# A Fourier mixer and a SoLU layer on one core: the order of the opening's transfers, and the buffers and transfers of the last pairs

## The chip, the core and the metric

The kernel runs on one core of one Trainium2 chip. The time is device microseconds of one launch. The kernel before took 1618.07 us in the median of three runs (1616.99 to 1626.45); a profiled execution of it took 1612.3 us. Five engines work side by side, each through its own list of instructions in order: TensorE (PE, with PEld for its weight loads), VectorE (DVE), ScalarE (ACT), GpSimd (POOL) and SyncE (SP), which only issues transfers. They wait for one another through semaphores. In these traces a line such as L858 is a line of the kernel before.

## What is computed

```
X = np.fft.rfft(x, axis=1)                     # x: 8 x 3136 x 256
Y = X * (filt_r + 1j * filt_i)[None, :, :]
y = np.fft.irfft(Y, n=3136, axis=1)            # 25088 tokens of 256
h = y @ w_in                                   # 256 -> 1024
e = np.exp(h - max(h)); sm = e / (sum(e) + 1e-9)
solu = h * sm
ln = (solu - mean(solu)) / sqrt(var(solu) + 1e-6) * g_ln
out = ln @ w_out                               # 1024 -> 256
```

All in float32. `w_in`, `w_out` and `g_ln` come as float64 and are converted on the chip.

## The kernel before

**Two halves that overlap.** Each of the eight sequences is a Fourier transform of length 3136 = 49 x 64, done as products with small tables. A first product per piece (`first`, eight pieces of four columns) goes through a tensor in DRAM (`d1`) to change its layout. The spectrum is then treated in seven units (`Spectrum.units`): six of four rows and a last one of a single row. For each unit `forward` makes two PSUM tiles `pb`, `multiply` multiplies them by the filter into `pr` and `pi` (VectorE, with one sum on GpSimd), `inverse` makes `pc`, ScalarE copies it to `g`, and `store` writes `g` to `d2` in DRAM. A last product per piece (`back`, tiles `py`) reads `d2` back as `t4` and leaves tokens in `y`.

Tokens go in blocks of 128, two blocks to a pair, 98 pairs. `product` makes `h` (tiles `m`), `exponential`, `normalize`, `square` and `turn` make the SoLU and its transposed blocks (`turn`), `regroup` moves these by DMA into `solu_t`, `project_sums` makes the sums of `solu_t` that a product scheme of seven instead of eight blocks needs (`u1`, `u2`, the sum written over `solu_t`, `u4`; all on GpSimd), and `project` makes the seven products 1, 2, 6, 7, 5, 3, 4 of a pair into the PSUM tiles `o`. Between them `keep_out` (ScalarE, L871) and `finish_out` (VectorE, L875) empty the banks into `ot`, and `store_out` writes `ot` to the output. Products 6, 5 and (except in the last pairs) 3 add to the bank of product 1, so each waits for the `keep_out` before it; product 4 adds to the bank of 2 and 7 and waits for a `finish_out`.

**The opening.** Sequence 0 has nothing to overlap with. Everything stands in an order written by hand (`manual_schedule`). SP's transfers there are, in order: eight parts of unit 0's rows (L563), the rows of units 1 and 2 (`y<-d`, L295, 512 KB each, into a free part of `y`), the last tables (`load_tables(8, ...)`: `de`, 640 KB, and eight filter pieces of 128 or 160 KB), the rows of units 3 to 6, and then `t4` in eight pieces. ScalarE issues the stores of `g`; GpSimd issues the raw weights (`begin`, 512 KB each) one after each unit's sum. In the loop over the units, TensorE runs `forward` two units ahead: pb of unit 3, pc of unit 1, pb of unit 4, pc of unit 2 and so on. The tiles `pr`, `pi` and `g` have two buffers each. After the last unit fourteen products whose results nobody reads (`idle_row(14, "idler")`) keep TensorE running until the first `t4` piece is there. Each `t4` piece has 100 rows: 96 from units 0 to 5 and 4 from unit 6, and `by_16` fetches them as two transfers.

**The semaphores of transfers.** In the built program the transfers of SP and ACT share eight semaphores in turn. Each transfer carries a wait for the landing of the one that used its semaphore before it; the issuing engine stands at that wait.

**The end.** `last` holds the pairs 93 to 97. Their stores are issued by GpSimd, except those of pair 97 (SP). `ot` has two buffers, so pair 96 uses that of pair 94. SP regroups pairs 96 and 97 one after the other in step k = 198; pair 97 uses two of the four buffers of pool `r`.

Of the kernel before, what the change touches and what calls it, by code (L numbers as in the profile page):

```python
# [9 lines left out]
FP32 = mybir.dt.float32  # L10
# [7 lines left out]
P = 128  # L18
B, S, C = 8, 3136, 256
# [6 lines left out]
NS, NQ = (N1 + 1) // 2, 64  # L26
NP = (NS + 1) // 2
NR = 2 * N1
NK = 4 * NS
# [65 lines left out]
def kernel(  # L95
# [31 lines left out]
    d1 = [dram.tile([NS, P, C], FP32, name=f"d1_{e}") for e in range(B)]  # L127
    d2 = [dram.tile([NS, P, C], FP32, name=f"d2_{e}") for e in range(B)]
    f_dram = dram.tile([NP, 2, NQ, 2, C], FP32, name="f_dram")

# [57 lines left out]
    class Spectrum:  # L188
# [156 lines left out]
        def store(self, i, dma):  # L345
            rows, n = self.rows(i, d2[self.e])
            dma(out=rows, in_=self.gs.pop(i)[:, 0:n, :])

    t4s = {}

    def fetch_first_back(ch):
        by_16((nc.sync.dma_start, nc.sync.dma_start), t4s[0, ch],
              d2[0].rearrange("s (a n) c -> (s a) n c", a=4)[:, NCH * ch:NCH * ch + NCH, :])

# [51 lines left out]
    with ExitStack() as st:  # L406
# [158 lines left out]
        for i in range(1, units):  # L565
            sp.fetch(i, nc.sync.dma_start, spare_piece(i - 1))
            if i == 2:
                load_tables(8, NP - 8, nc.sync.dma_start)
        for i in range(2):
            start(i)  # L570
        for i in range(units):
# [13 lines left out]
            elif i != 2:  # L585
                begin({1: 2, 3: 3, 4: 4, 5: 5, 6: 6}[i])
        idle_row(14, "idler")
        rows_t4 = pools["r"].tile([P, NH, C], FP32, name="t4_0", tag="r")
# [96 lines left out]
    def load_de(sp, u):  # L685
# [5 lines left out]

    turns, variances, solu_ts, solu_sums, spreads, rss, pos, ots, places = (
        {} for _ in range(9))
    sums, ms, hs, nmaxs, es, solus, squares = {}, {}, {}, {}, {}, {}, {}
# [99 lines left out]

    def regroup(p, i):


        g, second = divmod(p, 2)
        turned = turns[g].rearrange("p (k q) b i -> p k q (b i)", q=4)
        a = 2 * second + i  # L800
        if p == last[-1]:
            st = pools["r"].tile([P, KF, P], FP32, name=f"solu_t_{p}_{i}", tag="r")
        else:
            st = upool.tile([P, KF, P], FP32, name=f"solu_t_{p}_{i}", tag=f"solu_t{i}")
        solu_ts[p, i] = st[:, 0:KF // 2, :], st[:, KF // 2:KF, :]
        for q in range(4):
            nc.sync.dma_start(out=st[32 * q:32 * q + 32, :, :],  # L807
                              in_=turned[32 * a:32 * a + 32, :, q, :])

# [54 lines left out]
    def out_half(p, i, n):  # L864
        if p not in ots:
            ots[p] = wk2.tile([P, 2, C], FP32, name=f"ot_{p}", tag="ot")
        return ots[p][:, i, P * n:P * n + P], rss[p // 2][:, 2 * (p % 2) + i:2 * (p % 2) + i + 1]
# [10 lines left out]
    def store_out(p):  # L878
        g, second = divmod(p, 2)

        rows = out[4 * P * g:4 * P * g + 4 * P, :].rearrange("(b a i) c -> a b i c", a=4, i=32)
        for i in range(2):
            (nc.gpsimd if p in last[:-1] else nc.sync).dma_start(out=rows[2 * second + i], in_=ots[p][:, i, :])
        del ots[p]
# [79 lines left out]
    def step(k):  # L964
# [23 lines left out]
        if not odd:  # L988
# [37 lines left out]
            if 0 <= j - 3 < pairs - 1:  # L1026
                for n in range(j - 3, pairs if j - 3 == pairs - 2 else j - 2):
                    regroup(n, 0)
                    regroup(n, 1)
            if 0 <= j - 4 < pairs:  # L1030
# [16 lines left out]
        else:  # L1047
# [6 lines left out]
            if proj:  # L1054
                project(p, 1)
                keep_out(p, 0, (0, 0))
                project(p, 2)
                finish_out(p, 0, 0, (0, 0), 1)
# [17 lines left out]
            if proj:  # L1076
                keep_out(p, 1, (1, 0))
            if 3 <= k < blocks + 3:
                square(k - 3)
# [45 lines left out]
```

## Time and profile before

| what | us |
|---|---|
| median of three runs | 1618.07 |
| the profiled execution | 1612.3 |
| its span, first to last instruction | 1610.2 |
| mean granted clock of TensorE | 0.991 of full |

| stretch of the span, us | length | PE busy | granted clock | DMA share |
|---|---|---|---|---|
| 0 to 53: first products, tables, unit 0 | 53.0 | 33.17 | 0.90 | 0.94 |
| 53 to 105: units 1 to 6, unread products, `back` | 52.0 | 45.47 | 0.93 | 0.80 |
| 105 to 142: the first steps | 37.0 | 33.15 | 0.96 | 0.79 |
| 142 to 1571.8: the steps | 1429.8 | 1412.28 | 1.00 | 0.69 |
| 1571.8 to 1605.5: the last three pairs | 33.7 | 28.57 | 0.90 | 0.43 |

PE busy is the time in which TensorE has a product in flight; the granted clock is the share of the full clock that the throttle let through; the DMA share is the mean busy share of the core's 16 DMA engines. A wait in a profile is written as waiting engine and line, arrow, what ended the wait. A letter q behind an engine is its issuing part: SPq L807 is SP issuing a transfer. Between the span and the execution's time lie 2.1 us.

### The profile page before, as it was taken

The numbers are of one execution on the slowest core, as the hardware profiler recorded it, in microseconds if no ns is written. First come the engines' busy times: TensorE is split into PE (matmuls) and PEld (weight loads), VectorE is DVE, ScalarE is ACT, GpSimd is POOL, SyncE is SP. The second block draws the span as 40 slices with busy tenths as digits, with TensorE's granted clock in tenths as the row PEclk, the third lists the DMA queues.
The fourth block names the chain that finished last, engine by engine and source line by source line (L and its number), as shares of the span: only waits on it lengthen the run. The fifth ranks groups of instructions, "written<-read, shape, count | busy, mean of one in ns | idle before, by whom it ended". The sixth has DMA issues, their size and how long they took to land.

```text
span 1610.2 us, 37028 instructions
## 1 busy us (share of the span) xinstructions
PE 1552.6 (96%) x12808; PEld 1057.4 (66%) x12808; DVE 1316.2 (82%) x2635; ACT 913.2 (57%) x1821; POOL 1196.3 (74%) x1386
## 2 busy tenths in 40 slices
PE   5798899999999999999999999999999999999997
PEld 1362456666666676667766676667767777777776
DVE  1687887898899889987999789987898777777772
ACT  2135555566656656666565655666555665666662
POOL 4446998679777876886778877797776767677775
PEclk8999999999999999999999999999999999999999
DMA  9888878786887679866886678766774545344343
GB/s 274 245 267 246 251 219 237 210 228 199 216 258 235 180 200 257 236 181 164 229 240 206 169 194 254 202 189 176 219 222 125 141 118 133 86 113 110 106 112 99
DMA packets 342651, 311.94 MB, mean 194 GB/s; under 512 B 28922, under 2 KB 307987, under 8 KB 342467
## 3 DMA queue, kind: packets, MB, share of 16 engines
q1 hardware_dynamic: 268724, 167.37, 39.5%
q0 software_dynamic: 35648, 102.76, 21.1%
q10 hardware_dynamic: 38096, 39.46, 8.2%
q8 instruction: 104, 1.70, 0.5%
q14 instruction: 79, 0.65, 0.1%
HBM read 124.78 MB, written 81.40 MB: 128 GB/s over the span
## 4 chain that ended last, share of the span: by engine, by line
PE 66%; DMA 2%; DVE 1%; issue 1%; POOL 0%; SPq 0%; ACT 0%; DVEq 0%; POOLq 0%; ACTq 0%
PE o L858 30%; PE m L728 28%; PE py L376 3%; PE pc L305 2%; PE pa L273 2%; PE pb L305 2%; DMA solu_t<-turn 1%; DMA x<-in_x_dram 1%; DVE h L776 0%; DMA out_dram<-ot 0%; PE o L822 0%; DVE h L752 0%; SPq L807 0%; POOL u L707 0%; DVE h L749 0%
## 5 line engine op out<-in xcount | busy, mean ns | idle before, releaser
L858 PEld LDWEIGHTS o<-w_out_sb,solu_t 128*128 128x128 f32 x3136 | 382.4, 192 | 49.6 <-issue 43.5
L858 PE MATMUL o<-w_out_sb,solu_t 128*128 128x128 f32 x3136 | 402.2, 276 | 3.4 <-DVE ot L875 2.6
L728 PE MATMUL m<-w_in_sb,s 128*128 128x512 f32 x784 | 398.0, 608 | 3.4 <-ACT h L738 1.6
L858 PEld LDWEIGHTS o<-w_out_sb,u 128*128 128x128 f32 x2352 | 307.5, 192 | 141.8 <-issue 105.4
L776 DVE SCALAR_TENSOR_TENSOR h<-e,rsum,h 128x1024 f32<-128x1024 f32 x196 | 320.5, 1635 | 6.9
L858 PE MATMUL o<-w_out_sb,u 128*128 128x128 f32 x2352 | 311.8, 276 | 4.9 <-ACT ot L871 4.8
L728 PE MATMUL m<-w_in_sb,y 128*128 128x512 f32 x588 | 308.4, 608 | 5.0 <-DVE nmax L752 3.5
L738 ACT COPY h<-m 128x512 f32<-128x512 f32 x294 | 173.2, 589 | 203.3 <-PE m L728 194.2
L871 ACT ACTIVATE ot<-o,rs_t 128x128 f32<-128x128 f32 x392 | 143.2, 367 | 253.3 <-PE o L858 244.0
L707 POOL TENSOR_TENSOR u<-solu_t 128x512 f32<-128x512 f32 x98 | 137.8, 1406 | 165.5 <-DMA solu_t<-turn 114.5
L784 ACT ACTIVATE h<-h,nmu 128x1024 f32<-128x1024 f32 x196 | 224.8, 1147 | 48.6 <-DVE turn L792 38.1
L792 DVE STREAM_TRANSPOSE turn<-h 128x1024 f32<-128x1024 f32 x196 | 243.1, 1240 | 3.1
L752 DVE CUSTOM_DVE_ANT_0 h<-m,h 128x512 f32<-128x512 f32 x196 | 133.3, 680 | 128.1 <-ACT h L738 97.9
L760 ACT ACTIVATE e<-h,nmax 128x1024 f32<-128x1024 f32 x196 | 225.1, 1148 | 21.2 <-DVE h L776 19.8
L707 POOL TENSOR_TENSOR u<-solu_t,u 128x512 f32<-128x512 f32 x98 | 149.2, 1522 | 93.6 <-PE o L858 93.6
L728 PEld LDWEIGHTS m<-w_in_sb,s 128*128 128x128 f32 x784 | 127.8, 190 | 88.8 <-issue 67.1
L875 DVE SCALAR_TENSOR_TENSOR ot<-o,rs_t,ot 128x128 f32<-128x128 f32 x299 | 103.7, 347 | 78.4 <-ACT ot L871 59.9
L707 POOL TENSOR_TENSOR solu_t<-solu_t,solu_t 128x512 f32<-128x512 f32 x98 | 165.9, 1693 | 0.9
L728 PEld LDWEIGHTS m<-w_in_sb,y 128*128 128x128 f32 x588 | 96.6, 191 | 101.6 <-issue 55.6
L707 POOL TENSOR_TENSOR u<-u,solu_t 128x512 f32<-128x512 f32 x98 | 150.8, 1538 | 15.6 <-PE o L858 8.1
L707 POOL TENSOR_TENSOR s<-y 128x128 f32<-128x128 f32 x196 | 96.5, 493 | 0.5
L376 PEld LDWEIGHTS py<-wb_t,t 50*64 50x64 f32 x3584 | 57.6, 134 | 42.9 <-issue 19.4
(123 smaller groups left out, 2020.6 us busy)
## 6 DMA issues: line engine op xcount, KB each, us to landing
solu_t<-turn SPq DMA_DIRECT2D x784, 128.0 KB
out_dram<-ot SPq DMA_DIRECT2D x188, 128.0 KB
t<-d POOLq DMA_DIRECT2D x112, 200.0 KB, 6.9
d<-x POOLq DMA_DIRECT2D x100, 200.0 KB, 5.6
f<-f_dram POOLq DMA_DIRECT2D x39, 512.0 KB, 8.1
d<-g POOLq DMA_DIRECT2D x39, 512.0 KB, 5.0
t<-d ACTq DMA_DIRECT2D x37, 512.0 KB
x<-in_x_dram SPq DMA_DIRECT2D x112, 98.0 KB
```

The lines of the kernel that those rows point to most:

```text
L376: nc.tensor.matmul(out=views[g][64 * h:64 * h + 64, cb, i, :], lhsT=t4[rows, i, c0:c0 + 64], rhs=wb_t[rows, 0:N1], start=True, stop=True)
L707: nc.gpsimd.tensor_tensor(out=out, in0=in0, in1=in1, op=op)
L728: nc.tensor.matmul(out=ms[j, bank], lhsT=lhsT, rhs=w_in_sb[:, w, :], start=m in (1, 2, 7), stop=True, skip_group_check=True)
L738: nc.scalar.copy(out=h_half(k, i), in_=ms[j, 0])
L752: nc.vector.tensor_tensor_reduce(out=h_half(k, i), in0=ms[j, bank], in1=h_half(*kept), scale=1.0, scalar=sofar, op0=ALU.add, op1=ALU.min, ...
L760: nc.scalar.activation(out=e, in_=hs[k], func=AFT.Exp, bias=nmaxs.pop(k)[:, 1:2], scale=-1.0, accum_out=esum)
L776: nc.vector.scalar_tensor_tensor(out=solu, in0=e, scalar=rsum, in1=solu, op0=ALU.mult, op1=ALU.mult, accum_out=nmu)
L784: nc.scalar.activation(out=solu, in_=solu, func=AFT.Square, bias=nmu, scale=-float(DFF), accum_out=variances[g][:, i:i + 1])
L792: nc.vector.transpose(out=turns[g][:, :, i, :], in_=solus[k].rearrange("p (f j) -> p f j", j=32))
L858: nc.tensor.matmul(out=pos[p, bank], lhsT=lhs[:, f, :], rhs=w[:, f, :], start=f == 0 and (m in (1, 2, 7) or alone), stop=True, skip_group_ ...
L871: nc.scalar.activation(out=out_half(p, *to)[0], in_=pos[p, 0], func=AFT.Copy, scale=rs)
L875: nc.vector.scalar_tensor_tensor(out=ot, in0=pos[p, bank], scalar=rs, in1=out_half(p, *kept)[0], op0=ALU.mult, op1=ALU.add)
```

## The change

It has two places.

In the opening, the last tables are issued when i is 3, so after the rows of units 1, 2 and 3. The last unit's result goes to a DRAM tensor of its own, `d2_last`. `fetch_first_back` takes the 96 rows from `d2` and the four from `d2_last`, and for the first two pieces the order is: 96 rows of piece 0, 96 of piece 1, four of piece 0, four of piece 1. Eleven unread products stand where fourteen stood.

At the end, all stores are issued by SP, those of pairs 93 to 96 too. `ot` of pairs 96 and 97 comes from pool `r`. `regroup` can do some of its four parts and on another queue: SP regroups pairs 96 and the first block of 97; the four parts of the second block of 97 are issued by ScalarE in step k = 199, two behind the `keep_out` of product 1 of pair 95, and two behind that of its product 6. In the built program nothing else moves on any engine, and the number of transfers is the same: four fewer pairs of stores on GpSimd, four more on SP, four parts of a regroup on ScalarE instead of SP.

```diff
@@ -126,6 +126,7 @@
 
     d1 = [dram.tile([NS, P, C], FP32, name=f"d1_{e}") for e in range(B)]
     d2 = [dram.tile([NS, P, C], FP32, name=f"d2_{e}") for e in range(B)]
+    d2_last = dram.tile([1, P, C], FP32, name="d2_last")
     f_dram = dram.tile([NP, 2, NQ, 2, C], FP32, name="f_dram")
 
     wf_t = consts.tile([NR, NK], FP32, name="wf_t")
@@ -344,13 +345,18 @@
 
         def store(self, i, dma):
             rows, n = self.rows(i, d2[self.e])
+            if self.e == 0 and n == 1:
+                rows = d2_last.rearrange("s p c -> p s c")
             dma(out=rows, in_=self.gs.pop(i)[:, 0:n, :])
 
     t4s = {}
 
     def fetch_first_back(ch):
-        by_16((nc.sync.dma_start, nc.sync.dma_start), t4s[0, ch],
-              d2[0].rearrange("s (a n) c -> (s a) n c", a=4)[:, NCH * ch:NCH * ch + NCH, :])
+        for rest in range(2):
+            d, place = ((d2[0][0:NS - 1], slice(0, NK - 4)), (d2_last, slice(NK - 4, NK)))[rest]
+            for n in ([0, 1] if ch == 0 else [ch] if ch > 1 else []):
+                nc.sync.dma_start(out=t4s[0, n][place], in_=d.rearrange("s (a n) c -> (s a) n c", a=4)[
+                    :, NCH * n:NCH * n + NCH, :])
 
     def fetch_back(e, ch):
 
@@ -564,7 +570,7 @@
                 out=t2_0[NH * (n % 4):NH * (n % 4) + NH, n // 4, :], in_=rows_x[n:n + 1])
         for i in range(1, units):
             sp.fetch(i, nc.sync.dma_start, spare_piece(i - 1))
-            if i == 2:
+            if i == 3:
                 load_tables(8, NP - 8, nc.sync.dma_start)
         for i in range(2):
             start(i)
@@ -584,7 +590,7 @@
                 nc.gpsimd.dma_start(out=g_sb, in_=moe_g_ln.rearrange("(k p) -> p k", p=P))
             elif i != 2:
                 begin({1: 2, 3: 3, 4: 4, 5: 5, 6: 6}[i])
-        idle_row(14, "idler")
+        idle_row(11, "idler")
         rows_t4 = pools["r"].tile([P, NH, C], FP32, name="t4_0", tag="r")
         for ch in range(pieces):
             t4s[0, ch] = rows_t4[0:NK, NCH * ch:NCH * ch + NCH]
@@ -689,8 +695,8 @@
                             in_=de_dram[i:i + pairs].rearrange("i p k u q -> p i (k u q)"))
         return de
 
-    turns, variances, solu_ts, solu_sums, spreads, rss, pos, ots, places = (
-        {} for _ in range(9))
+    turns, variances, solu_ts, solu_sums, spreads, rss, pos, ots, places, regrouped = (
+        {} for _ in range(10))
     sums, ms, hs, nmaxs, es, solus, squares = {}, {}, {}, {}, {}, {}, {}
 
 
@@ -792,20 +798,21 @@
         nc.vector.transpose(out=turns[g][:, :, i, :],
                             in_=solus[k].rearrange("p (f j) -> p f j", j=32))
 
-    def regroup(p, i):
+    def regroup(p, i, dma=nc.sync.dma_start, parts=range(4)):
 
 
         g, second = divmod(p, 2)
         turned = turns[g].rearrange("p (k q) b i -> p k q (b i)", q=4)
         a = 2 * second + i
-        if p == last[-1]:
-            st = pools["r"].tile([P, KF, P], FP32, name=f"solu_t_{p}_{i}", tag="r")
-        else:
-            st = upool.tile([P, KF, P], FP32, name=f"solu_t_{p}_{i}", tag=f"solu_t{i}")
-        solu_ts[p, i] = st[:, 0:KF // 2, :], st[:, KF // 2:KF, :]
-        for q in range(4):
-            nc.sync.dma_start(out=st[32 * q:32 * q + 32, :, :],
-                              in_=turned[32 * a:32 * a + 32, :, q, :])
+        if (p, i) not in regrouped:
+            if p == last[-1]:
+                st = pools["r"].tile([P, KF, P], FP32, name=f"solu_t_{p}_{i}", tag="r")
+            else:
+                st = upool.tile([P, KF, P], FP32, name=f"solu_t_{p}_{i}", tag=f"solu_t{i}")
+            regrouped[p, i] = st
+            solu_ts[p, i] = st[:, 0:KF // 2, :], st[:, KF // 2:KF, :]
+        for q in parts:
+            dma(out=regrouped[p, i][32 * q:32 * q + 32, :, :], in_=turned[32 * a:32 * a + 32, :, q, :])
 
     def deviations(g):
         rs = small.tile([P, 4], FP32, name=f"rs_{g}", tag="rs", bufs=2)
@@ -863,7 +870,10 @@
 
     def out_half(p, i, n):
         if p not in ots:
-            ots[p] = wk2.tile([P, 2, C], FP32, name=f"ot_{p}", tag="ot")
+            if p in last[-2:]:
+                ots[p] = pools["r"].tile([P, NCH, C], FP32, name=f"ot_{p}", tag="r")[:, 0:2]
+            else:
+                ots[p] = wk2.tile([P, 2, C], FP32, name=f"ot_{p}", tag="ot")
         return ots[p][:, i, P * n:P * n + P], rss[p // 2][:, 2 * (p % 2) + i:2 * (p % 2) + i + 1]
 
     def keep_out(p, i, to):
@@ -880,7 +890,7 @@
 
         rows = out[4 * P * g:4 * P * g + 4 * P, :].rearrange("(b a i) c -> a b i c", a=4, i=32)
         for i in range(2):
-            (nc.gpsimd if p in last[:-1] else nc.sync).dma_start(out=rows[2 * second + i], in_=ots[p][:, i, :])
+            nc.sync.dma_start(out=rows[2 * second + i], in_=ots[p][:, i, :])
         del ots[p]
 
     blocks = NT * B // 2
@@ -1026,7 +1036,8 @@
             if 0 <= j - 3 < pairs - 1:
                 for n in range(j - 3, pairs if j - 3 == pairs - 2 else j - 2):
                     regroup(n, 0)
-                    regroup(n, 1)
+                    if n != last[-1]:
+                        regroup(n, 1)
             if 0 <= j - 4 < pairs:
                 project_sums(j - 4, 1)
             if 0 <= j - 3 < pairs and j % 2:
@@ -1054,6 +1065,9 @@
             if proj:
                 project(p, 1)
                 keep_out(p, 0, (0, 0))
+            if j == pairs + 1:
+                regroup(last[-1], 1, nc.scalar.dma_start, range(2))
+            if proj:
                 project(p, 2)
                 finish_out(p, 0, 0, (0, 0), 1)
             if 2 <= k < blocks + 2:
@@ -1075,6 +1089,8 @@
                 normalize(k - 2)
             if proj:
                 keep_out(p, 1, (1, 0))
+            if j == pairs + 1:
+                regroup(last[-1], 1, nc.scalar.dma_start, range(2, 4))
             if 3 <= k < blocks + 3:
                 square(k - 3)
             for job in first_parts[k]:
```

## The prediction

> **What bounds the kernel now.** I read the page first: how busy each engine is, then the chain of work that ended last.
>
> ```profile
> PE 1552.6 (96%) x12808; PEld 1057.4 (66%) x12808; DVE 1316.2 (82%) x2635; ACT 913.2 (57%) x1821; POOL 1196.3 (74%) x1386
> ...
> PE 66%; DMA 2%; DVE 1%; issue 1%; POOL 0%; SPq 0%; ACT 0%; DVEq 0%; POOLq 0%; ACTq 0%
> ```
>
> TensorE is busy 96% of 1610.2 us. The change leaves every product of the long middle as it is, so only stretches in which TensorE stands still, or runs slowly, can move the time. The busy time by windows shows two of each (columns: window, its length, busy time of PE, PEld, DVE, ACT, POOL with instruction counts, granted clock, DMA share, GB/s).
>
> ```profile
> 53.00:57.80 4.80, 0.07 (x2) 0.02 (x1) 4.53 (x7) 1.07 (x2) 3.38 (x6) 0.90 0.89 266
> 57.80:63.70 5.90, 5.89 (x38) 2.71 (x42) 0.00 (x0) 0.00 (x0) 1.18 (x1) 0.50 0.84 282
> ...
> 1586.80:1591.30 4.50, 0.00 (x0) 0.00 (x1) 0.08 (x1) 0.37 (x1) 4.50 (x5) 0.80 0.74 192
> 1591.30:1596.30 5.00, 4.97 (x23) 5.00 (x24) 0.27 (x1) 0.37 (x1) 2.83 (x3) 0.50 0.36 88
> ```
>
> Each stop of 4.5 to 4.8 us is followed by 5 to 6 us at half clock. A stop therefore costs its length plus about half of the slow stretch: 4.7 + 2.9 = 7.6 us in the opening, 4.5 + 2.5 = 7.0 us at the end. These 14.6 us are the most that the change can win. Who ends them, from the waits of the opening (us in total, times, longest) and the timeline of the end:
>
> ```profile
> SPq L295 <- DMA d<-g: 9.2, 1, 9.2
> ```
>
> ```profile
> PE pb L305 <- DMA y<-d: 4.7, 1, 4.7
> ```
>
> ```profile
> 1583.85 1.45 POOL L883 DMA_DIRECT2D out_dram<-ot  x2
> ...
> 1590.82 0.37 ACT L871 ACTIVATE ot<-o,rs_t 128x128 f32<-128x128 f32 x1 [5.74 <-DMA out_dram<-ot]
> ...
> 1591.33 2.05 PE L858 MATMUL o<-w_out_sb,u 128*128 128x128 f32 x8 [4.56 <-ACT ot L871]
> ```
>
> The first stop waits for the rows of unit 3 (`y<-d`). SP issues them at 52.89, behind the last tables (42.60 to 52.85). The second is a buffer: `ot` of pair 96 needs the store of pair 94, which POOL issues only at 1583.85, after its sums and `rs`, `wide`, and which lands at 1590.6.
>
> [...] 0.50 from 56.89 to 63.71 and from 1589.47 to 1596.30, and a stop of 1.84 us at 136.7 inside a thin stretch also cost 3.41 us at half. [...] a regroup part from SP lands 2.4 us after its issue alone, and 4.8 to 6.5 us after it beside POOL's stores. [...] in the trace ACT's copies of `g` stand behind waits on their stores (4.4 us).
>
> **The change, part by part**
>
> *Unit 3's rows ahead of the tables.* SP issues y3 at 42.60, in the place of `de`. Units 1 and 2 (512 KB each) land at 46.5 and 47.9, 1.44 us apart, so y3 lands near 49.3. Pair product pb of unit 3 then follows pc of unit 0 at 53.1 instead of 57.8: **4.7 us earlier and at full clock**. What it is moved past is 1.4 us later: `de` and eight filter pieces, landing by 56.4 instead of 55.0; unit 4 multiplies with them only after 60, so that costs nothing. But two things are late next. Unit 4's rows wait in the built program for the third filter piece: issue near 54.2 (before 53.37), landing near 59.0. TensorE is through with pc of unit 1 at about 57.1: a stop of 1.9 us. And unit 5's rows now carry the wait that only the small unit 6 carried (the 9.2 us above): every transfer of SP and ACT waits for the landing of the earlier one that used its semaphore, and for unit 5 that is now unit 0's store. Before, this store was issued at 54.20 and landed at 63.6, behind three units' rows. Now it has only unit 4's rows ahead: two times 1.44 us after 57.6, about 60.5. Unit 5 then lands 2.8 us (unit 1's store, alone) to 4.8 us (unit 3's rows) later, 63.3 to 65.3, middle 64.2. Before, pb of unit 5 ran at 66.59. So the spectra end **2.4 us earlier** (bounds 4.7, no late row, and 0), not 7.6. [...] I take the clock as staying full, and keep the other answer for the bound of 0.
>
> *Last unit's result in its own place.* In the program before, the 96-row fetches wait for the stores of units 1 to 5 only, and the small 4-row ones for unit 6's store; 85.01 and 85.65 are their first issues. The own tensor removes no wait: **0**. The new order puts piece 1's 96 rows ahead of piece 0's last four: +1.6 us on the first piece (pieces land 1.4 to 1.7 us apart).
>
> *11 unread products for 14.* Each takes 0.86 us (28 matmuls in 12.04 us), so TensorE reaches the rows 2.6 us earlier: 78.32 - 2.4 + 9.5 = 85.4. This is a gain only where rows are there. Before, piece 0 landed at 90.1, TensorE began at 90.4. Rows are late because unit 5's store, issued at 77.15, lands at 84.9 behind weights 4, 5 and 6 of POOL (71.55, 74.71, 76.57). Weights 3 and 4 follow POOL's sums of units 3 and 4, which come 6 and 5 us earlier now, so two 512-KB transfers leave this crowd (before, landings there follow one another by 1.3 to 1.9 us). I take 2.8 us off that store beside the shift: 84.9 - 2.4 - 2.8 = 79.7; then 5.1 us to the first piece as before, +1.6: 86.5. TensorE waits 1.1 us (at 109.4 a stop of 1.24 us left the clock alone) and begins at 86.5: 3.9 us earlier. The next limit is DVE. Its weight conversions shift by the spectra's 2.4 us, and its first `h` at 111.19 frees the bank that a product at 112.4 needs, 0.5 us later than needed now. **Opening in sum: -2.9 us.**
>
> *Last pairs.* `ot` of pairs 96 and 97 take free buffers of pool r, so the second stop goes. Stores of pairs 93 to 96 leave POOL (0.7 us each, 1.4 for a pair) for SP, behind the regroups; nothing waits for those of 94 to 96 any more, and 93's two (1.3 us on SP) are out by 1574, before pair 96's regroup at 1577.81. Without POOL's store beside it, pair 95's regroup lands near 1574.1 instead of 1576.6, but TensorE waited only 0.4 us for those sums. What is late next is ACT. It now issues half of pair 97's regroup, four transfers of about 0.62 us, each waiting for a part of pair 96's regroup, which land at 1580.8, 1582.1, 1583.5 and 1584.8. Queued behind them are `ot` of pair 95: 1580.68 becomes about 1582.8, so the next product starts at 1583.2 instead of 1581.7; and those of 1582.80 become 1586, so pair 95's last product starts at 1587.0 instead of 1583.6. Pair 96's two products follow (2.0 us, with the turn of `rs` 0.2, their waits 1.0), and its product on `u2` starts at 1590.1 instead of 1591.33: 1.2 us. POOL's sums are ready by 1588. From there the clock is full: 2.2 us more. **End: -3.4 us.** Bounds: ACT free in time, -6.3 (`u2` at 1587.5, full clock); its stops also cool the clock, +1.
>
> *Sum:* -2.9 - 3.4 = -6.3. The profiled execution took 1612.3 us (span 1610.2): 1606.0 and 1603.9. The median of the runs, 1618.07, stands 5.8 above it; I forecast the median: **1612**.
>
> **Rivals**
> 1. *Both stops go and nothing takes their place*: -14.6 us, 1603.5. For it: both stops have one named cause each, and it is removed. Against: the built waits of unit 5's rows and of ACT. 10%.
> 2. *The waits only move*: unit 5 lands near 66 (-0.6) and ACT's waits grow until the end gains 0.4: -1, 1617. For it: the DMA share of 0.9 in the opening. 20%.
> 3. *Slower*: the eleven products end too early. If unit 5's store keeps its 7.8 us, piece 0 lands at 82.5 + 6.7 = 89.2, TensorE stands from 85.4, 3.8 us, and the 14.4 us of py begin at half clock: +2.5, so py ends at 106.1 instead of 104.9, +1.2. With ACT's stops cooling the clock at the end (+1): 1620. [...] For it: both long stops of today did this. Against: the weights leave the crowd. 13%.
> 4. *The change doesn't do what it says*: the own tensor, as shown; it is part of each case.
>
> **How the numbers follow.** My case has 57%: 1608 to 1616. The range must reach rivals 2 and 3 and most of the way to 1: **1604 to 1620**. About 1% (16 us) is what a measurement of this kernel tells from no change. All cases lie inside it: faster by more 0.06, within 0.90, slower by more 0.04, the ends for runs that scatter (1616.99 to 1626.45 before).
>
> **What would show it.** pb of unit 3 at about 53 without a wait on `y<-d`; SP waiting on `d<-g` ahead of unit 5's rows; a stop of one to two microseconds ahead of pb of units 4 and 5; the first py near 86.5 with a stop under 2 us; no wait of ACT on `out_dram<-ot` at the end, but waits on `solu_t<-turn` of about 2 us each ahead of `ot` of pair 95. I am wrong if TensorE runs at half clock after 60, if py begins later than 88.5, or if ACT does not wait.

## The result and the profile after

| | before | after |
|---|---|---|
| median, us | 1616.51 (6 runs) | 1623.24 (6 runs, 1621.15 to 1635.44) |
| ratio, 95% interval | | 1.0054, 1.0030 to 1.0078 |
| the profiled execution; its span | 1612.3; 1610.2 | 1623.3; 1621.2 |
| start of the first back product (`py`) | 90.44 | 94.18 |
| start of the first product of `h` | 104.71 | 121.57 |
| start of the last product of `h` | 1564.22 | 1578.90 |
| end of the last product | 1605.09 | 1616.11 |

The kernel after is slower: its median by 6.7 us, by the interval of the ratio 4.8 to 12.6 us. The two profiled executions, from which the lower rows come, differ by 11.0. Read down these rows: 3.7 us are lost before the back products, 13.1 more within them, 2.2 come back in the steps, and 3.7 at the end. (The profiled execution after was 1.5 us late already at pb of unit 0, before anything that the change touches.)

The page, engine shares and then the chain of waits, shows next to nothing of this: TensorE's share rose, since slow work is busy work.

```profile
PE 1565.5 (97%) x12802; PEld 1072.2 (66%) x12802; DVE 1319.0 (81%) x2635; ACT 911.8 (56%) x1821; POOL 1181.7 (73%) x1378
...
PE 65%; DMA 3%; DVE 1%; issue 1%; SPq 0%; ACT 0%; POOL 0%; ACTq 0%; DVEq 0%; POOLq 0%
```

The busy time by windows of the kernel after (columns as in the prediction) shows it at once, in the granted clock:

```profile
53.00:58.40 5.40, 4.95 (x42) 2.69 (x42) 5.33 (x9) 1.12 (x3) 4.66 (x7) 1.00 0.83 160
58.40:63.40 5.00, 0.00 (x0) 0.01 (x1) 3.67 (x6) 1.02 (x2) 2.41 (x2) 0.90 1.01 356
63.40:69.30 5.90, 5.88 (x38) 2.71 (x42) 0.00 (x0) 0.00 (x0) 0.61 (x2) 0.50 0.77 269
...
90.30:94.20 3.90, 0.06 (x2) 0.05 (x1) 3.76 (x7) 0.00 (x0) 0.98 (x1) 0.86 1.03 240
94.20:121.80 27.60, 27.60 (x129) 27.60 (x130) 18.71 (x31) 7.28 (x15) 4.47 (x3) 0.50 0.79 263
```

The first stop of before, for unit 3's rows, is gone: TensorE works through 53 to 58. It has moved to unit 4 (5.10 us for 4.74), with as long a slow stretch behind it. The last two lines are new: a stop of 3.9 us, and then the whole stage of back products at half clock. TensorE was never idle in it. The same stage in the kernel before:

```profile
90.40:104.90 14.50, 14.50 (x130) 14.50 (x130) 14.15 (x25) 7.30 (x15) 3.09 (x3) 1.00 0.82 227
```

The timeline of the kernel after at its end (start, length, engine, line, what was done; in brackets the idle time and what ended it) answers to the stop at 1591.33 in the prediction:

```profile
1597.59 0.37 ACT L881 ACTIVATE ot<-o,rs_t 128x128 f32<-128x128 f32 x1 [3.71 <-DMA solu_t<-turn]
...
1598.01 3.44 PE L865 MATMUL o<-w_out_sb,u 128*128 128x128 f32 x16 [1.97 <-ACT ot L881]
...
1600.98 0.63 ACT L881 ACTIVATE ot<-o,rs_t 128x128 f32<-128x128 f32 x2 [3.02 <-DMA solu_t<-turn]
```

No wait on `out_dram` is left. ScalarE now stands behind its own transfers, which wait for parts of pair 96's regroup, and TensorE waits 2 us for ScalarE where it waited 4.6.

### The profile page after: what moved, and what is told of

It is laid out like the page before. It is cut to its first block, busy times and chain, and to the rows that moved or that the text cites. A ratio compares the mean times of both kernels' runs of the same rounds, so it can differ in the third digit from the quotient of the medians.

```text
span 1621.2 us, 37010 instructions
## 1 busy us (share of the span) xinstructions
PE 1565.5 (97%) x12802; PEld 1072.2 (66%) x12802; DVE 1319.0 (81%) x2635; ACT 911.8 (56%) x1821; POOL 1181.7 (73%) x1378
## 4 chain that ended last, share of the span: by engine, by line
PE 65%; DMA 3%; DVE 1%; issue 1%; SPq 0%; ACT 0%; POOL 0%; ACTq 0%; DVEq 0%; POOLq 0%
PE o L865 29%; PE m L734 28%; PE py L382 3%; PE pc L306 2%; PE pa L274 2%; PE pb L306 2%; DMA solu_t<-turn 1%; DMA x<-in_x_dram 0%; DMA out_dram<-ot 0%; DMA t<-d 0%; DVE h L782 0%; SPq L815 0%; PE o L829 0%; DVE h L758 0%; DVE h L755 0%
## 5 line engine op out<-in xcount | busy, mean ns | idle before, releaser
L713 POOL TENSOR_TENSOR u<-solu_t 128x512 f32<-128x512 f32 x98 | 133.9, 1366 | 177.9 <-DMA solu_t<-turn 119.7
L713 POOL TENSOR_TENSOR u<-solu_t,u 128x512 f32<-128x512 f32 x98 | 145.8, 1488 | 89.1 <-PE o L865 89.0
L713 POOL TENSOR_TENSOR u<-u,solu_t 128x512 f32<-128x512 f32 x98 | 154.6, 1577 | 14.2 <-PE o L865 5.8
```

The costliest lines, as they stand in the source:

```text
L713: nc.gpsimd.tensor_tensor(out=out, in0=in0, in1=in1, op=op)
```

## The experiments

The theory from these lines: three unread products fewer leave a stop ahead of the back products, the clock falls, and these products do not bring it back. "The stage" means the eight pieces of back products, from the first of them to the first product of `h`. The rivals: the back products are slow for another reason (the order of their rows, their transfers), or the loss comes from the stop ahead of unit 4. "Changed kernel" is the kernel after.

### How many unread products

```diff
-        idle_row(11, "idler")
+        idle_row(14, "idler")
```

> The changed kernel with fourteen unread products for eleven, nothing else. Theory (H1: three products fewer leave a stop of 3.84 us ahead of the first back product, the clock falls, and the short back products do not bring it back, so the stage takes 27.6 us for 14.4): the stop shrinks to about 1.3 us, the clock stays full through the back products, they take about 14.5 us, and the time is about 1610 us, 13 us below the changed kernel. Rival A (the back products are slow for another reason, such as the new order of their rows): they still take about 27 us, time 1620 to 1624. Rival B (the loss comes from the stop ahead of unit 4): no change, 1623.

Ratio to before 1.0009 (0.9990 to 1.0027), median 1616.64 of 20. The profile:

```profile
93.64 14.50 PE L405 MATMUL py<-wi_t,t 100*128 100x98 f32 x128 [0.58 <-DMA t<-d_last]
```

The new order of rows is still in, and the stage takes 14.5 us at a granted clock of 1.00: rival A falls. The stop ahead of unit 4 is there too (5.21 us): rival B falls. The time, though, is some 7 us below the changed kernel, where 13 were expected. The other way round, eleven for fourteen in the kernel before:

> The kernel before with eleven unread products for fourteen, nothing else. The stop ahead of the first back product grows from about 0.1 us to about 2.7 us. H1 in its strong form (any stop there makes the clock fall): the back products take about 27 us, time about 13 us above before, 1629. H1 with a threshold [...]: clock full, time equal to before within 1 us. Rival A (the slow back products come from the new order of rows): equal to before.

Ratio 1.0027 (1.0007 to 1.0048), median 1622.10 of 20.

```profile
90.21 26.61 PE L399 MATMUL py<-wi_t,t 100*128 100x98 f32 x128 [2.07 <-DMA t<-d]
```

This one edit makes the slow stage in the old kernel: the granted clock is 0.52 from 90.20 to 116.80. A stop of 2.07 us was enough, not the 3.8 of rival 3. But the times of these 20 executions run from 1609.67 to 1631.16. Each execution has its mean granted clock beside its time. 26.6 us at 0.52, as in this profile, take 26.6 x 0.48 / 1620 = 0.008 off the mean. I divide at 0.9855. The profiled executions of all kernels agree with that: the five with the slow stage have a mean of 0.979 to 0.984, the others 0.985 or more. For executions without a profile it is inferred from the mean.

| kernel | stop ahead of `py` in its profile, us | executions at 0.985 or less | their median | median of the others |
|---|---|---|---|---|
| before (all runs beside the experiments) | 0.0 | 9 of 248 | 1625.51 | 1615.97 |
| changed, 14 products | 0.58 | 4 of 20 | 1628.11 | 1615.42 |
| before, 11 products | 2.07 | 11 of 20 | 1626.89 | 1615.95 |
| changed, its pieces in order (below) | 1.62 | 8 of 9 | 1625.70 | 1618.69 (one) |
| changed | 3.84 | 6 of 6 | 1623.24 | none |

So the loss is a draw, made anew in each execution, and in these runs its odds moved with the number of unread products (4 of 20 for fourteen, 6 of 6 for eleven in the changed kernel). What decides between executions of one kernel is not shown. Within one kernel it costs 9.5 (1625.51 - 1615.97) to 12.7 us (1628.11 - 1615.42), the row with a single other execution left out. The profiles say a little more: 27.60 - 14.43 = 13.2.

### The order of the first pieces

```diff
-        for rest in range(2):
-            d, place = ((d2[0][0:NS - 1], slice(0, NK - 4)), (d2_last, slice(NK - 4, NK)))[rest]
-            for n in ([0, 1] if ch == 0 else [ch] if ch > 1 else []):
+        for n in [ch]:
+            for rest in range(2):
+                d, place = ((d2[0][0:NS - 1], slice(0, NK - 4)), (d2_last, slice(NK - 4, NK)))[rest]
```

> The changed kernel with the first piece's own four rows fetched right behind its 96 rows (piece by piece), nothing else; still eleven unread products. If the order costs what I put down (+1.6 us on the first piece): the stop ahead of the back products shrinks from 3.84 us to about 2.2 us. That is as long as the 2.07 us that let the clock fall with eleven products in the opening of before, so the clock most likely still falls and the time stays within 3 us of the changed kernel, 1620 to 1623; if a stop of 2.2 us can leave the clock alone in some runs, some are 13 us shorter.

Ratio 1.0046 (1.0024 to 1.0067).

```profile
93.56 26.46 PE L405 MATMUL py<-wi_t,t 100*128 100x98 f32 x128 [1.62 <-DMA t<-d]
```

The stop is 1.62 us, 2.2 less than in the changed kernel's profile. The order makes 1.35 us of that: from the issue of the first piece's 96 rows to the landing of its last part 5.28 us pass here (88.03 to 93.31) and 6.63 there (87.41 to 94.04). Most of the rest is unit 5's store, which took 6.89 us here and 7.87 there. The stop varies as much from one execution to the next: five profiles below, of kernels that are the changed one up to this point, have stops of 2.50 to 4.29 us. The clock fell all the same: the stage took 26.46 us for 14.50 with fourteen products, and the execution's mean clock is 0.981.

### What brings the clock back

Four unread products behind the first back piece of the changed kernel:

```diff
                 back(0, ch, cb, nc.scalar.copy)
+            if ch == 0:
+                idle_row(4, "dense")
```

> The changed kernel with four more unread products of 512 columns, put behind the first piece of the back products (work is added). H1: at half clock the four take about 7 us, the clock comes back during or right after them, the other seven pieces take 12.6 us instead of some 24, so the stage with the four is about 22 to 24 us instead of 27.6, and the time some 4 to 6 us below the changed kernel: about 1618. Rival A (back products slow for another reason than the clock): +3.5 to +7 us, 1627 to 1630.

Ratio 1.0013 (0.9999 to 1.0028), median 1619.03: with work added, 4.2 us below the changed kernel. Busy time by windows, back products of piece 0 first, then the four, then the rest:

```profile
92.70:96.20 3.50, 3.46 (x16) 3.49 (x17) 3.47 (x6) 0.49 (x1) 1.47 (x1) 0.50 1.03 253
96.20:99.50 3.30, 3.30 (x6) 1.43 (x5) 3.20 (x7) 0.49 (x1) 0.19 (x1) 0.50 1.03 283
99.50:101.30 1.80, 1.80 (x5) 0.76 (x4) 1.73 (x4) 0.00 (x0) 0.00 (x0) 1.00 0.70 207
101.30:113.90 12.60, 12.60 (x114) 12.59 (x113) 11.54 (x19) 6.33 (x13) 2.81 (x2) 1.00 0.66 245
```

The granted clock is 0.50 from 92.70 to 99.50, 6.8 us with the first 3.3 us of the dense products in it, then 1.00; the back products then keep it full (1.00 over 12.6 us). In the traces of the kernels before and after, each stretch at half clock that ends inside the execution lasts 3.41 us or a multiple of it: 10.24, 6.83, 3.41 and 6.83 before, 13.65, 6.83, 30.72, 6.83 and 3.41 after. The expectations that follow call 3.41 us a window. I took the shortness of the back products for the reason: 98 columns to a weight load. The next run puts short products there.

```diff
+            for j in range(21 if ch == 0 else 0):
+                nc.tensor.matmul(out=ps_h.tile([P, 2, C], FP32, name=f"short_{j}", tag="h")[:, :, 0:49],
+                                 lhsT=tables[0][0][:, 0, 0].rearrange("p u q -> p (u q)"),
+                                 rhs=filters[0][0][:, 0][:, :, 0:49], start=True, stop=True)
```

> The changed kernel with 21 more unread products of 98 columns behind the first back piece: as many columns as the four of 512 in the dense run, but each with a weight load of its own, like the back products, and with operands that are long there. Theory (it is the shortness of the products per weight load that keeps the clock from coming back): the clock stays at half through all of the stage, which takes 27.4 + 21 x 0.2156 = 31.9 us, and the time is 3 to 6 us above the changed kernel, about 1627. Rival (it is something particular to the back products, such as their rows or the emptying of their banks, and any other work brings the clock back): full clock after one or two windows as in the dense run, stage about 22 us, time about 1618.

```profile
97.20:102.50 5.30, 5.30 (x26) 5.30 (x26) 5.16 (x11) 0.49 (x1) 0.86 (x1) 0.50 0.85 208
102.50:104.40 1.90, 1.90 (x19) 1.90 (x18) 1.80 (x4) 0.00 (x0) 0.54 (x1) 0.99 0.46 172
104.40:117.00 12.60, 12.60 (x115) 12.60 (x115) 7.84 (x13) 6.32 (x13) 1.40 (x1) 1.00 0.75 280
```

Shortness alone is not the reason: the granted clock is 0.50 up to 102.50, 5.3 us into the short products, and 0.99 behind it, and no execution of 20 has the low mean clock. (The median, 1622.53, ratio 1.0027, 1.0012 to 1.0042, moved less than expected; what I conclude rests on the clock.) What was left are three differences of the back products, taken in three runs: 100 of 128 rows in use, their own operands (on 100 rows too), their strided place in the bank (on 128).

```diff
-                                 lhsT=tables[0][0][:, 0, 0].rearrange("p u q -> p (u q)"),
-                                 rhs=filters[0][0][:, 0][:, :, 0:49], start=True, stop=True)
+                                 lhsT=tables[0][0][0:NK, 0, 0].rearrange("p u q -> p (u q)"),
+                                 rhs=filters[0][0][0:NK, 0, :, 0:49], start=True, stop=True)
```

> The changed kernel with the 21 unread products of 98 columns behind the first back piece, as in the short run, but on 100 rows of their operands for 128, as the back products. If the number of rows in use is what keeps the clock down: half clock through the whole stage, first back product to first product of h about 32 us. If not: full clock within three windows of 3.41 us as in the short run, stage about 23 us.

```diff
+                                 lhsT=t4s[0, 0][:, j % 4, 0:P], rhs=wi_t, start=True, stop=True)
```

> The same, but the 21 unread products read what the back products read (the first piece's 100 rows and their table) and write to a plain place of a bank. If rows or operands decide: half clock through the stage, about 32 us. If it is the strided place or the emptying of the banks: full clock within three windows, about 23 us.

```diff
-                nc.tensor.matmul(out=ps_h.tile([P, 2, C], FP32, name=f"short_{j}", tag="h")[:, :, 0:49],
+                ps = ps_h.tile([P, 512], FP32, name=f"short_{j}", tag="h")
+                i = j % 4
+                nc.tensor.matmul(out=ps[:, 0:NCH * NR].rearrange("p (m r) -> p m r", r=N1)[
+                                     :, i:2 * NCH - i:2 * NCH - 1 - 2 * i, :],
```

> The same with the operands of the short run (128 rows) but written to the strided place in the bank that the back products use. If the place decides: half clock through the stage, about 32 us. If rows or operands decide: full clock within three windows, about 23 us.

Windows over the unread products and what follows them: the rows alone first, then the place alone.

```profile
96.90:105.80 8.90, 8.90 (x43) 8.90 (x43) 8.62 (x16) 0.49 (x1) 1.39 (x1) 0.50 0.77 214
105.80:129.80 24.00, 24.00 (x115) 24.00 (x114) 7.43 (x13) 6.32 (x13) 1.41 (x1) 0.50 0.56 214
```

```profile
94.70:98.40 3.70, 3.70 (x19) 3.70 (x19) 3.60 (x7) 0.49 (x1) 0.63 (x1) 0.50 1.02 249
98.40:101.20 2.80, 2.80 (x27) 2.80 (x27) 2.73 (x6) 0.00 (x0) 0.00 (x0) 1.00 1.03 246
```

On 100 rows the clock is 0.50 from 96.90 to 129.80, 32.9 us with the same products and the rest of the stage in them, and with the back products' own operands it is 0.50 in the same 32.9 us again; on 128 rows, in the strided place, it is 1.00 from 98.40, 7.0 us after the first back product (91.37). Of the three differences the rows decided here; the first run differs from the short one in nothing else. (A stage of 35.4 us, not 32: each float32 product shows as two entries, so the 21 cost 42 x 0.218 us at half clock, twice what I had put down.) The times of the first two, 1638.21 and 1634.38, fit, but come from two executions each, all four with the low mean clock. The third does not fit: at 1623.86 (1.0054, 1.0032 to 1.0075) it is no faster than the changed kernel, though its stage took 22.3 us in the profile and that of the changed kernel 27.4. Where the rest went stays open.

The back products themselves on 128 rows, with zeros in the table's other 28:

```diff
-    wi_t = consts.tile([NK, NR], FP32, name="wi_t")
+    wi_t = consts.tile([P, NR], FP32, name="wi_t")
+    nc.vector.memset(wi_t[96:P], 0.0)
...
-            t4s[0, ch] = rows_t4[0:NK, NCH * ch:NCH * ch + NCH]
+            t4s[0, ch] = rows_t4[:, NCH * ch:NCH * ch + NCH]
+        nc.sync.dma_start(out=rows_t4[NK:P], in_=x[0, 0:(P - NK) * NH].rearrange("(p n) c -> p n c", n=NH))
```

> The changed kernel whose back products use 128 rows for 100: the 28 more rows hold tokens of the input (one more transfer of 0.9 MB on SP ahead of the pieces) and meet zeros in the table, so the sums are the same; still eleven unread products. The transfer adds to the crowd, so the stop ahead of the back products will be as long as in the changed kernel or longer (4 to 8 us) and the clock falls. If the rows in use decide: the clock comes back within one to three windows of 3.41 us of the first back product, and the stage takes 16 to 20 us for 27.6. If not: half clock through the stage, 27 us.

Ratio 1.0026 (1.0013 to 1.0039).

```profile
94.56 14.69 PE L406 MATMUL py<-wi_t,t 128*128 128x98 f32 x128 [2.61 <-DMA t<-d_last]
```

The stop was 2.61 us, and the stage took 14.69 us, where it took 14.50 with the clock at 1.00 (fourteen products): the clock did not fall in the profile. Of the 20 executions 2 have a mean clock of 0.985 or less, where the changed kernel had 6 of 6. But this profile has no fallen clock ahead of these products, so a last run made the stop longer (six unread products):

> The last run's kernel with six unread products for eleven, so that TensorE stands some 6 to 7 us ahead of the back products and the clock falls for certain. If the rows in use decide: back products begin at half clock and full clock is back one to three windows of 3.41 us after the fall has ended, stage 16 to 20 us, then full. If not: half clock through the stage, 27 us.

```profile
94.33 17.21 PE L406 MATMUL py<-wi_t,t 128*128 128x98 f32 x128 [3.62 <-DMA t<-d_last]
```

The granted clock is 0.50 from 93.20 to 99.90, 6.7 us, and 0.99 in the 10.1 us behind them; the stage took 17.2 us where the changed kernel's took 27.6 behind a stop of nearly the same length. (The stop is not 6 us, since the spectra ended later in this execution.) Ratio 1.0012 (0.9986 to 1.0038).

Rows are not the whole of it, as the traces of both kernels show at their beginning. There TensorE runs the first products (`pa`) and nothing else, on 98 rows, but with 512 columns to a weight load. From the kernel before, the first 24 entries of them, then two pairs of weight loads that follow one another:

```profile
8.36 12.95 PE L230 MATMUL pa<-x,wf_t 98*100 98x512 f32 x24 [8.36 <-DMA x<-in_x_dram]
...
10.19 0.29 PEld L230 LDWEIGHTS pa<-x,wf_t 98*100 98x100 f32 x1 [0.56 <-issue]
11.04 0.29 PEld L230 LDWEIGHTS pa<-x,wf_t 98*100 98x100 f32 x1 [0.56 <-DMA x<-in_x_dram]
...
15.10 0.17 PEld L230 LDWEIGHTS pa<-x,wf_t 98*100 98x100 f32 x1 [0.26 <-issue]
15.53 0.17 PEld L230 LDWEIGHTS pa<-x,wf_t 98*100 98x100 f32 x1 [0.26 <-issue]
```

They follow one another every 0.85 us at first, so at half clock, and every 0.43 us later. The trace's record of the clock begins with full clock at 12.51. (The views count the time ahead of that record as full clock, so the 0.90 given for the first stretch of the kernel before is too high.) In the kernel after the same record begins at 14.64, with the first of them at 10.17. So these products on 98 rows had full clock 4.15 and 4.47 us after the first of them. The runs show something narrower than "the rows decide": of products with 98 columns, those on 128 rows had the clock back 3.7 to 5.6 us after the first of them (three profiles), and those on 100 rows still ran at half clock when their stages ended, 26.2 to 35.8 us long (five profiles).

One measure puts these cases in order, rows times columns per ns at half clock, an estimate of mine from the ns between starts. The kernel after has 213 for the back products, 853 for the first products and 853 for the first products of `h`; the run with the longer stop has 26 entries in 5.57 us at half clock, 214. That makes 100 x 98 / 213 = 46 for the back products, behind which the clock stayed at half; 128 x 98 / 214 = 59 for those on 128 rows, 98 x 512 / 853 = 59 for the first products and 128 x 512 / 853 = 77 for the products of `h`, during which it came back. No run was made to test this measure.

### Unit 3's rows alone

```diff
-            if i == 2:
+            if i == 3:
                 load_tables(8, NP - 8, nc.sync.dma_start)
```

> The kernel before with the rows of unit 3 ahead of the last tables, alone; fourteen unread products. Theory (the move only hands the stop on to unit 4, whose rows then land late): pb of unit 3 without a wait near 53, a stop of 4 to 5 us ahead of pb of unit 4 with half clock behind it, pb of unit 5 within 1.5 us of before, back products at full clock in about 14.4 us, and the time within 2 us of before. My prediction's step said 2.4 us earlier for pb of unit 5.

Ratio 0.9987 (0.9974 to 1.0000). Timeline of TensorE:

```profile
60.95 1.12 PE L305 MATMUL pb<-y,de 64*64 64x256 f32 x16 [2.77 <-DVE pr L328]
66.07 1.12 PE L305 MATMUL pb<-y,de 64*64 64x256 f32 x16 [1.90 <-DMA y<-d]
```

pb of unit 5 comes 0.5 us earlier than before, not 2.4. The stop divides between units 4 and 5, and here both parts left the clock full (1.00 from 61.00 to 64.10 and from 66.10 to 69.00).

### The end

The end alone (the hunks from `turns, variances` on, with the opening of before):

> The kernel before with the end of the change alone (stores of the last pairs by SP, ot of the last two pairs from pool r, half of the last regroup on ScalarE); the opening is that of before. By the trace of the changed kernel the end is worth -3.65 us: time about 1613 (before 1616.5), the opening's back products at full clock in 14.5 us. Rival (the end's waits on ScalarE give the gain back): within 1 us of before.

Ratio 0.9984 (0.9967 to 1.0002), median 1613.29 against 1616.45. From the start of the last product of `h` to the end of the last product: 37.23 us, in the changed kernel 37.22, in before 40.87. The end is worth 3.6 us, with TensorE's stop of 1.97 us behind ScalarE still in it. With the regroup all on SP:

```diff
-                    if n != last[-1]:
-                        regroup(n, 1)
+                    regroup(n, 1)
...
-            if j == pairs + 1:
-                regroup(last[-1], 1, nc.scalar.dma_start, range(2))
...
-            if j == pairs + 1:
-                regroup(last[-1], 1, nc.scalar.dma_start, range(2, 4))
```

> The kernel before with the end of the change, but with all eight parts of the last pair's regroup on SP, as before; ScalarE issues none. Theory (ScalarE's waits for the landing of pair 96's regroup, behind which its emptying of pair 95's banks queues, are what keeps the end from gaining more): no stop of about 2 us ahead of the product on u of pair 96, and the end gains 5 to 6.3 us against before instead of 3.7. Rival (the late thing is the regroup itself or POOL's sums, so who issues the last four parts is all one): the end gains 3 to 4 us again, with the stop ended by a DMA or by POOL.

Ratio 0.9961 (0.9943 to 0.9979): faster than before. The same stretch is 35.37 us, a gain of 5.5. The timeline of this run:

```profile
1598.74 1.16 PE L859 MATMUL o<-w_out_sb,u 128*128 128x128 f32 x8 [1.46 <-POOL u L707]
```

ScalarE's wait is gone; what comes late next is GpSimd's sums of pair 96.

### Versions meant to beat both

All have the end on SP; all but the last have the pieces of before and no `d2_last`. The first also fills the stop of the spectra with pc of units 1 and 2, put ahead of pb of units 3 and 4, with eighteen unread products:

```diff
-            if i + 2 < units:
+            if i + 2 < units and i not in (1, 2):
                 start(i + 2)
...
             sp.store(i, nc.scalar.dma_start)
+            if i in (1, 2):
+                start(i + 2)
...
-        idle_row(14, "idler")
+        idle_row(18, "idler")
```

> A version meant to beat both: opening of before, but with pc of unit 1 put ahead of pb of unit 3 and pc of unit 2 ahead of pb of unit 4 on TensorE, so that the stop for the rows of unit 3 is filled with work that is ready; eighteen unread products so that the rows of the back products are there when they end; the end as in the run with all of the regroup on SP. If the order of TensorE is what made the stop cost its length: stop below 2 us, no half clock at 57 to 64, spectra 3 to 5 us earlier, back products warm, opening -1 to -3 us, end -4 to -6: 1608 to 1611. Rival (rows of units 4 and 5 are the bound whatever TensorE does): opening 0 to +2, total equal to the run with the end alone.

Ratio 0.9959 (0.9941 to 0.9976), median 1611.30 of 13. From 50 to 72 the products were slow between 60.42 and 64.15 only (`pb` at 60.42 took 2.01 us, at 68.79 1.12), but pb of unit 5 came at 68.79 behind a stop of 2.62 us for its rows, and `py` at 95.69: the rival is right, the rows are the bound and the gain is the end's. Unit 3's rows first, with fourteen unread products:

> Unit 3's rows first (fourteen unread products, pieces of the back products as before) together with the end whose regroup is all on SP. If the two gains add: -1.8 (the rows' run) and -6.3 (the end's run) against before, so some 1609 to 1611, ratio about 0.995; no stop above 1.3 us ahead of the back products, so full clock there. Rival (the gain of the rows was chance): the ratio of the end alone, 0.996.

Ratio 0.9979 (0.9964 to 0.9995), median 1612.10: the gains do not add. In the profile unit 4's stop was 7.96 us. With four unread products in that stop:

```diff
-            sp.forward(i, halves(f"pb_0_{i}"))
+            pb = halves(f"pb_0_{i}")
+            for _ in range(4 if i == 4 else 0):
+                idle(pb[0])
+            sp.forward(i, pb)
```

> The same with four unread products of 512 columns ahead of pb of unit 4, where TensorE stands for 3 to 5 us. If the stop's second cost (5.9 us at half clock) can be had back by work that fills it: no half clock between 57 and 70, 0 to 3 us below the version without them, 1606 to 1610. Rival (the clock was full there in most runs anyway, and rows that come early wait for the filler): 0 to +1.5 us against it.

Ratio 0.9963 (0.9948 to 0.9977), median 1610.00: 2.1 us below the version without them, which the overlapping intervals don't settle, and with a granted clock of 1.00 from 53 to 90 in the profile. Last, the changed kernel with fourteen products and the end on SP:

> The changed kernel with two of its parts set back: fourteen unread products, and the regroup of pair 97 all on SP; d2_last, the order of the first pieces, unit 3's rows first and the buffers and stores of the end stay. Theory: stop ahead of the back products about 0.5 us, clock full, and the end some 2 us shorter than in the changed kernel: 1608 to 1612, 12 to 15 us below the changed kernel. Rival: the loss of the changed kernel lies elsewhere, then it stays above 1618.

Ratio 1.0003 (0.9982 to 1.0023), median 1615.67: a miss (1608 to 1612 was expected). 4 of 22 executions have the low mean clock (median 1627.24), and the others are at 1614.41. The version with unit 3's rows first and fourteen products, run beside it, differs from it in two things only: it has neither the own tensor nor the new order of the first pieces. It is at 1612.10, and none of its 22 executions has the low mean clock. The runs with the change's own tensor and order and fourteen products have it in 8 of 42 executions (4 of 20 with fourteen products alone, 4 of 22 here), those with unit 3's rows first but without these two parts in 0 of 42. So with the two parts together the slow stage came more often even behind fourteen products. Whether they also cost time at full clock, 1614.41 against 1612.10, the scatter does not settle. The two profiles do not show it either: the back products begin at 93.18 here and at 94.98 there, behind stops of 6.08 and 7.96 us for unit 4's rows.

Of the versions, the first three and the end with its regroup on SP, with ratios of 0.9959 to 0.9979, are faster than both kernels and can't be told apart.

## Why the prediction was wrong

I forecast 1612; it is 1623.24, above the range. Rival 3, given 13%, described the opening, but priced it far too low. Of the three signs of being wrong two came: half clock after 60 (62.42 to 69.25) and `py` later than 88.5 (94.18).

- **The failed step** is "11 unread products for 14", in two terms. First, "I take 2.8 us off that store": unit 5's store took 7.87 us from issue to landing (79.46 to 87.33), 7.78 before. No weight had left the crowd. The last three were issued 5.5, 2.3 and 0.5 us ahead of the store, and 5.6, 2.4 and 0.6 before. The first of them follows GpSimd's sum of unit 4, which I had 5 us earlier; it came 2.4 us later than before (72.77 for 70.33), because unit 4's rows were late:

```profile
72.77 1.27 POOL L329 TENSOR_TENSOR pi<-pi,pt 128x512 f32<-128x512 f32 x1 [8.76 <-PE pb L306]
73.98 0.78 POOL L421 DMA_DIRECT2D raw<-in_moe_w_out_dram  x1
```

The first piece was complete at 94.04, not 86.5, and TensorE stopped 3.84 us, not 1.1; rival 3 said 3.8. Second, the price of such a stop. My own case put it at nothing, and rival 3 at "the 14.4 us of py begin at half clock: +2.5". I took 2.5 us as the whole of it. In the profile none of the stage's products brought the clock back, which was 0.50 from 93.14 to 123.86, into the products of `h`; that cost 13.2 us in the profile, 9.5 to 12.7 between executions. Nor did it need a stop of 3.8 us: the clock fell behind 1.62 and 2.07 us, and 8 of 9 and 11 of 20 executions of those kernels have the low mean clock.
- **Unit 3's rows.** pb of unit 3 came without a wait at 53.5 (forecast 53.1), and SP stood at unit 0's store before unit 5's rows, as forecast, but until 62.57 and not 60.5. Unit 4's rows, issued at 56.01, landed at 63.34, not 59.0: I used the 1.44 us between landings of an uncrowded stretch. The stop was 5.10 us, not 1.9, and the clock did not stay full (0.50 from 62.42 to 69.25). Alone, the move gains 0.5 us of 2.4.
- **The own tensor at nothing, its order at 1.6.** The first piece's 96 rows were issued at 87.41, right behind the landing of unit 5's store at 87.33. The order delayed the first piece by 1.35 us, near the forecast. What I left out is that the slow stage comes more often with the two together (8 of 42 executions for 0 of 42).
- **DVE as the next limit.** From the first product of `h` to the 29th entry of such products before took 35.60 us, after 33.74. That this is VectorE giving time back is not shown: two kernels with the opening of before took 34.28 and 38.28 us there.
- **The end, -3.4.** It is -3.65 in the trace, step by step as argued. Set back by 14.68 us, the distance of the two traces at the last product of `h`, the product behind ScalarE's first wait starts at 1583.33 (forecast 1583.2), pair 95's last at 1587.10 (1587.0), that on `u2` at 1590.12 (1590.1). ScalarE's waits were longer than the 2 us put down, 3.71 and 3.02 us.

The sum: 9.5 to 12.7 for the slow stage and -3.6 for the end make 5.9 to 9.1, around the measured 6.7. What the other parts add the interval (4.8 to 12.6 us) does not resolve.

That copies on ScalarE stand behind the transfers that the same engine issues ahead of them shows at the end of the kernel after: the copies into `ot` wait there for parts of the regroup, 3.71 and 3.02 us. The 4.4 us of the copies of `g` in the prediction can be a wait for a buffer alone.

## What to carry to other kernels

Before you take away work that only keeps TensorE running, look at what comes behind it. Here back products on 100 rows did not bring the clock back, and a stop of two microseconds nearly doubled the stage (14.4 to 26.6 us behind 2.07 us); the odds of that stop are what to design for. Read the granted clock of every execution as well as of the profiled one; a median over two kinds of executions hides both. Where a stage has short products on part of the rows, begin it warm, or fill the other rows so that they meet zeros, as in the two runs with 128 rows (stages of 14.69 and 17.21 us for 27.60), and measure what the filling costs.

## What the runs showed of the hardware

- Products of 98 columns on 128 rows had full clock again 5.3 us after the first of them (short products), after 3.7 us (the same in the strided place) and after 5.6 us (back products on 128 rows behind the longer stop). Products of 98 columns on 100 rows did not have it: 0.50 over 27.6 us in the kernel after, 0.52 over 26.6 us in that of before with eleven products, 0.50 over 32.9 us in the run on 100 rows and in that with their own operands. Products of 512 columns on 98 rows had it 4.15 and 4.47 us after the first of them (kernels before and after), those on 128 rows after 3.3 us (the dense ones). Products of 98 columns on 100 rows kept a clock that was full (14.5 us at 1.00 in the kernel before and with fourteen products).
- Stops of 1.6 to 2.8 us ahead of busy stretches went either way: full clock behind 1.90 and 2.77 us (unit 3's rows alone) and 2.61 (back products on 128 rows), half clock behind 1.62 (pieces in order), 2.07 (before, 11 products), 2.50 (strided place) and 2.64 (dense products).
- Half clock came in multiples of 3.41 us in the traces of the kernels before and after (3.41, 6.83, 10.24, 13.65, 30.72), but for the last piece, which the end cuts off.
